# A decode attention kernel bound by its loads: paired transposes of K, other last parts of V, and the result on two partition quadrants

## The chip, the cores and the metric

The kernel runs on one core of one Trainium2 chip. The metric is the time on the device in microseconds (us); lower is better. All runs quoted here were timed beside runs of the kernel before on the same chip.

## The reference, cut to what matters

One decode step: attention of one new token over a long cache, plus a feed-forward block, for 4 batches and 32 heads.

```python
B, D, H, Sk, Dh, F = 4, 512, 32, 8192, 128, 1792        # all tensors bf16
xn = layernorm(x)                                       # x: [4, 1, 512]
q  = (xn @ wq) -> [B, H, 1, Dh]
p  = softmax(einsum("bhqd,bhkd->bhqk", q, k_cache) * Dh ** -0.5)
o  = einsum("bhqk,bhkd->bhqd", p, v_cache)              # k_cache, v_cache: [4, 32, 8192, 128]
return x + o @ wo + (silu(xn @ w_gate) * (xn @ w_up)) @ w_down
```

K and V are 268 MB each and every element is used once, so nearly all of the kernel is the reading of 551 MB.

## The kernel before: the parts concerned

There are 64 tiles of K and 64 of V, 4 MB each: one batch and two heads, with 128 rows of T = 128 keys. Five slots in SBUF, the on-chip memory, hold them. All loads go out on one queue. A round takes one K tile in eight pieces, and the V tile of two rounds earlier.

```python
def load_v(n, parts=(T,)):              # the last V tiles come in parts
    ...
    for w in parts:
        c1 = c0 + w * Dh
        nc.sync.dma_start(out=t_[:, c0:c1], in_=src[:, c0:c1])
        c0 = c1

def t_piece(n, g):                      # VectorE turns one eighth of a K tile
    w = TG * Dh
    kt = kt_pool.tile([P, w], dt.bfloat16, name="kt")
    src = k_tiles[n][:, g * w:(g + 1) * w].bitcast(dt.uint32)
    nc.vector.transpose(out=kt[:].bitcast(dt.uint32).rearrange(...), in_=src.rearrange(...))
    kts[n, g] = kt

def s_piece(n, g):                      # TensorE: scores, four matmuls per piece
    ...
    for jp in range(4):
        mm(s_ps[gr][:], zq[gr % 2][:, bb, jp, off:off + P], kt[:, jp // 2, :, jp % 2], ...)

def pv_last(xps, ts):                   # the last V tile: one small matmul per key column
    ...
def fin_2(j, xps, nb=B, start=True):    # adds the other three batches of the last head pair
    mm(xps[:, :, 0:nb], osb.pop(j)[:], rowy[:, :, 0:nb], start=start)

def wo_mm(i):                           # output projection of head i, halves in two PSUM banks
    for half in range(2):
        mm(yo_ps[half][0:B, :], otn[:, i, :], wo_t[0][:, i * D + half * DH:i * D + (half + 1) * DH], start=False)

# ... main loop over 66 rounds; cut: softmax, PV, feed-forward
load_v(nv, (32, 32, 32, 16, 16) if nv == NT - 1 else (32,) * 4 if nv == NT - 2 else (T,))
for g in range(NTG):
    t_piece(i, g)
    s_piece(i, g)
...
pv_last(xps, range(T // 2)); fin_2(...); pv_last(xps, range(T // 2, T)); fin_3(...)   # last round
...
nc.vector.tensor_copy(out=res[0][:], in_=yo_ps[0][0:B, :])
nc.sync.dma_start(out=out_flat[:, 0:DH], in_=res[0][:])
nc.scalar.copy(out=res[1][:], in_=yo_ps[1][0:B, :])
nc.scalar.dma_start(out=out_flat[:, DH:D], in_=res[1][:])
```

Of the kernel before, what the change touches and what calls it, by code (L numbers as in the profile page):

```python
# [8 lines left out]
dt = mybir.dt  # L9
# [6 lines left out]
def kernel(  # L16
# [13 lines left out]
    nc = tc.nc  # L30
    P = nc.NUM_PARTITIONS
# [10 lines left out]
    NT = M // HT  # L42
# [2 lines left out]
    NQ = P // QB  # L45
    TG = 16
    NTG = T // TG
    NV = 512 // Dh
    SLOT = T * Dh
    NSLOT = 5  # L50
# [11 lines left out]
    slots = ctx.enter_context(tc.tile_pool(name="slots", bufs=NSLOT))  # L62
    const = ctx.enter_context(tc.tile_pool(name="const", bufs=1))
    persist = ctx.enter_context(tc.tile_pool(name="persist", bufs=1))
    kt_pool = ctx.enter_context(tc.tile_pool(name="ktp", bufs=5))
    pp = ctx.enter_context(tc.tile_pool(name="pp", bufs=2))
    small = ctx.enter_context(tc.tile_pool(name="small", bufs=2))
    psS = ctx.enter_context(tc.tile_pool(name="psS", bufs=2, space=bass.MemoryType.PSUM))
    psO = ctx.enter_context(tc.tile_pool(name="psO", bufs=1, space=bass.MemoryType.PSUM))
    psM = ctx.enter_context(tc.tile_pool(name="psM", bufs=1, space=bass.MemoryType.PSUM))  # L70
    psX = ctx.enter_context(tc.tile_pool(name="psX", bufs=1, space=bass.MemoryType.PSUM))
    psY = ctx.enter_context(tc.tile_pool(name="psY", bufs=2, space=bass.MemoryType.PSUM))
    ctx.enter_context(tc.manual_schedule())

    def mm(out_ap, lhsT, rhs, start, **kw):
        nc.tensor.matmul(out_ap, lhsT=lhsT, rhs=rhs, start=start, stop=True,  # L76
                         skip_group_check=True, **kw)
# [125 lines left out]
    otn = persist.tile([P, H, B], dt.bfloat16, name="otn")  # L203

    DH = D // 2
    yo_ps = [psY.tile([B, DH], dt.float32, name="yo_ps") for _ in range(2)]
    ffn = {}

    def load_ffn():
# [9 lines left out]
    def do_ffn():  # L219
        wg, wu, wd = ffn["w"]  # L220

        gu_ps = psM.tile([P, 2, FC * B], dt.float32, name="mps")
        for i, w in enumerate((wg, wu)):
            for fc in range(FC):
                for c in range(EC):
                    mm(gu_ps[:, i, fc * B:(fc + 1) * B], w[:, c, fc:F:FC], xnt_w[:, c, 0:B],
                       start=(i == 0 and fc == 0 and c == 0))
        eg = persist.tile([P, FC * B], dt.float32, name="eg")
        nc.scalar.activation(out=eg[:], in_=gu_ps[:, 0, :], func=ACT.Exp, scale=-1.0)
        nc.vector.tensor_scalar(out=eg[:], in0=eg[:], scalar1=1.0, scalar2=None, op0=ALU.add)  # L230
        sig = persist.tile([P, FC * B], dt.float32, name="sig")
        nc.vector.reciprocal(out=sig[:], in_=eg[:])
        gs = persist.tile([P, FC * B], dt.float32, name="gs")
        nc.vector.tensor_tensor(out=gs[:], in0=gu_ps[:, 0, :], in1=sig[:], op=ALU.mult)
        ht = persist.tile([P, FC * B], dt.bfloat16, name="ht")
        nc.vector.tensor_tensor(out=ht[:], in0=gs[:], in1=gu_ps[:, 1, :], op=ALU.mult)
        yf_ps = psM.tile([B, D], dt.float32, name="mps")
        for fc in range(FC):
            mm(yf_ps[0:B, :], ht[:, fc * B:(fc + 1) * B], wd[:, fc, :], start=(fc == 0))
        nc.vector.tensor_tensor(out=yfx[:], in0=yf_ps[0:B, :], in1=xf[:], op=ALU.add)  # L240

        for j in range(2):
            mm(yo_ps[j][0:B, :], ident_f[0:B, 0:B], yfx[:, j * DH:(j + 1) * DH], start=True)



# [22 lines left out]
                out=zq[gr % 2][a * QB:(a + 1) * QB, :, :, XO + a * QB].rearrange("p b (j r) -> p r j b", r=2),  # L269
                in_=qt[a * QB:(a + 1) * QB, half, :, hh * 2:hh * 2 + 2, cg * B + bp * 2:cg * B + bp * 2 + 2])  # L270

    def t_piece(n, g):

        w = TG * Dh
        kt = kt_pool.tile([P, w], dt.bfloat16, name="kt")
        src = k_tiles[n][:, g * w:(g + 1) * w].bitcast(dt.uint32)
        nc.vector.transpose(out=kt[:].bitcast(dt.uint32).rearrange("p (j t r) -> p t j r", j=2, r=QB),  # L277
                            in_=src.rearrange("p (t j r) -> p t j r", j=2, r=QB))
        kts[n, g] = kt

    def s_piece(n, g):
        gr, bb = divmod(n, 2)
        if bb == 0 and g == 0:
            s_ps[gr] = psS.tile([P, 512], dt.float32, name="sps")
        kt = kts.pop((n, g))[:].rearrange("p (j n r) -> p j n r", j=2, r=2)
        off = XO - 2 * (bb * NTG + g)
        for jp in range(4):
            mm(s_ps[gr][:], zq[gr % 2][:, bb, jp, off:off + P], kt[:, jp // 2, :, jp % 2],
               start=(bb == 0 and g == 0 and jp == 0))
# [6 lines left out]
    def max_2(gr):  # L296

        mps = psM.tile([P, 512], dt.float32, name="mps")
        nc.tensor.matmul(mps[:, 0:P], lhsT=nmx.pop(gr)[:, 0:1].to_broadcast([P, P]), rhs=ident_f[:, :],  # L299
                         is_transpose=True, start=True, stop=True, skip_group_check=True)  # L300
        nm = small.tile([P, HT, 2], dt.float32, name="nm")
        nc.vector.tensor_reduce(out=nm[:], in_=by_row(mps[:, 0:P]), axis=AX.XY, op=ALU.max, negate=True)  # L302
        nc.vector.tensor_tensor(out=nm[:], in0=nm[:], in1=rowb_q[:], op=ALU.mult)
        nb = small.tile([P, 1], dt.float32, name="nb")
        nc.vector.reduce_sum(out=nb[:], in_=nm[:], axis=AX.XY)
        p_ = pp.tile([P, 512], dt.bfloat16, name="p_")
        rs = small.tile([P, 1], dt.float32, name="rs")
        nc.scalar.activation(out=p_[:], in_=s_ps.pop(gr)[:], func=ACT.Exp, bias=nb[:, 0:1], scale=qscale,
                             accum_out=rs[:])
        pt[gr] = p_  # L310
        rs_t[gr] = (rs, mps)
# [37 lines left out]
               start=(t == 0))  # L349

    def fin_1(j):
        o_sb = pp.tile([P, NV, Dh], dt.float32, name="o_sb")
        nc.scalar.copy(out=o_sb[:].rearrange("p u d -> p (u d)"), in_=o_acc[j % 2][:])  # L353
        nc.vector.tensor_tensor(out=o_sb[:], in0=o_sb[:], in1=rowu[:].unsqueeze(2).to_broadcast([P, NV, Dh]), op=ALU.mult)  # L354
        o1 = pp.tile([P, Dh], dt.float32, name="o1")
        nc.vector.reduce_sum(out=o1[:], in_=o_sb[:].rearrange("p u d -> p d u"), axis=AX.X)  # L356
        osb[j] = o1
# [20 lines left out]
                                    in1=r_[q0:q1, y, :].unsqueeze(1).to_broadcast([QB, 4, B]), op=ALU.mult)  # L378

    def wo_mm(i):  # L380
        for half in range(2):
            mm(yo_ps[half][0:B, :], otn[:, i, :], wo_t[0][:, i * D + half * DH:i * D + (half + 1) * DH], start=False)

    NK = T // NV
    JL = H // HT - 2
# [3 lines left out]
    for i in range(NT + LP):  # L389

        if i + 2 < NT:
            load_k(i + 2)
        nv = i + 2 - LP
        if 0 <= nv < NT:
            load_v(nv, (32, 32, 32, 16, 16) if nv == NT - 1 else (32,) * 4 if nv == NT - 2 else (T,))
        if i == R_FFN - 3:
            load_ffn()
        if i == R_FFN:
            do_ffn()
        if i == R_WO - 2:  # L400
            load_wo()
        gr, bb = divmod(i, 2)
        if i < NT:
            for g in range(NTG):
                t_piece(i, g)
                s_piece(i, g)
                if g == 0 and bb == 0 and gr > 0:
                    pt_turn(gr - 1)
            if bb == 1:
                if gr + 1 < NT // 2:  # L410
                    build_q(gr + 1)
                max_1(gr)
        elif i == NT:
            pt_turn(NT // 2 - 1)
        npv = i - LP
        if npv == NT - 1:
            xps = x_tile()
            pv_last(xps, range(T // 2))
            fin_2(H // HT - 1, xps, nb=B - 1, start=False)
            pv_last(xps, range(T // 2, T))  # L420
            fin_3(H // HT - 1, xps)
            wo_ready = H
        elif npv >= 0:
            for k in range(NK):
                pv_chunk(npv, k)
                if k == 4 and i < NT and bb == 1:
                    max_2(gr)
            jv, bv = divmod(npv, B)
            if bv % 2 == 0:
                row_sums(npv // 2)  # L430
            if bv == B - 1 or npv == NT - 2:
                fin_1(jv)
            if bv == B - 1:
                if jv < JL:
                    fin_q(jv)
                    if jv % 2 == 1:
                        wo_ready = (jv + 1) * HT
                else:
                    xps = x_tile()
                    fin_2(jv, xps)  # L440
                    fin_3(jv, xps)
                    wo_ready = (jv + 1) * HT
        elif i < NT and bb == 1:
            max_2(gr)
        if i >= R_WO:
            for _ in range(8):
                if wo_next < wo_ready:
                    wo_mm(wo_next)
                    wo_next += 1
# [2 lines left out]
        wo_next += 1  # L452
    assert wo_next == H

    res = [persist.tile([B, DH], dt.bfloat16, name=f"res{j}") for j in range(2)]
    nc.vector.tensor_copy(out=res[0][:], in_=yo_ps[0][0:B, :])
    nc.sync.dma_start(out=out_flat[:, 0:DH], in_=res[0][:])
    nc.scalar.copy(out=res[1][:], in_=yo_ps[1][0:B, :])
    nc.scalar.dma_start(out=out_flat[:, DH:D], in_=res[1][:])


# [1 line left out]
_INS = ['A_x', 'A_k_cache', 'A_v_cache', 'A_wq', 'A_wo', 'B_x', 'B_w_gate', 'B_w_up', 'B_w_down']  # L463
_OUTS = [((4, 1, 512), 'bfloat16')]
# [25 lines left out]
```

## Time and profile before

| quantity | before |
|---|---|
| time, median of 3 runs | 1288.93 us (1288.82 to 1289.4) |
| span of the profiled run, mean granted TensorE clock (1 is full speed) | 1287.1 us, 0.933 |
| TensorE busy, VectorE busy | 84%, 57% of the span |
| load queue | 99.4% of 16 DMA engines |
| transposes of K | 512, some 1.14 us apart |
| last piece of V lands | 1282.67 us |
| output issued, span ends | 1285.00, 1287.11 us |

Read it from the load queue. A queue that is full for 99.4% of the span leaves nothing to win in the middle.

### The profile page before, as it was taken

How to read it: one execution, taken by the hardware profiler on the slowest of the kernel's cores; microseconds unless marked ns; L12 is line 12 of the kernel's file. 1: busy time of each engine (PE TensorE's matmuls, PEld its weight loads, DVE VectorE, ACT ScalarE, POOL GpSimd, SP SyncE). 2: the span in 40 equal slices, each digit the busy share in tenths (PEclk: the TensorE clock that was granted, in tenths of full speed). 3: DMA queues.
4: the chain of work that ended last, by engine and by line, in shares of the span. 5: the costliest groups of instructions: out<-in, count | busy, mean ns of one | idle time of the engine just before them, and what ended most of it. 6: DMA issues, size and time to landing. Idle time of an engine off the chain costs nothing.

```text
span 1287.1 us, 11189 instructions
## 1 busy us (share of the span) xinstructions
PE 1083.1 (84%) x4778; PEld 430.3 (33%) x4778; DVE 738.1 (57%) x951; ACT 39.7 (3%) x87; POOL 5.3 (0%) x13
## 2 busy tenths in 40 slices
PE   4888888888888798897997888888887988978788
PEld 1334333333333333332333333333333333333334
DVE  6663556546556556466556566465465465573544
ACT  1000000000000000000000000000000000000000
POOL 1000000000000000000000000000000000000000
PEclk9898898998989999898998989989899898989899
DMA  9999999999999999999999999999999999999997
GB/s 407 427 430 435 437 425 437 429 436 431 432 435 428 436 432 433 431 432 435 431 435 428 434 432 431 436 431 433 430 434 431 437 430 432 433 431 427 433 434 304
DMA packets 21529, 551.49 MB, mean 428 GB/s; under 512 B 2268, under 2 KB 2792, under 8 KB 3944
## 3 DMA queue, kind: packets, MB, share of 16 engines
q1 hardware_dynamic: 21464, 550.78, 99.4%
q8 instruction: 37, 0.61, 0.2%
q14 instruction: 12, 0.10, 0.0%
q10 hardware_dynamic: 16, 0.01, 0.0%
HBM read 550.77 MB, written 0.00 MB: 428 GB/s over the span
## 4 chain that ended last, share of the span: by engine, by line
DMA 50%; PE 31%; DVE 14%; issue 5%; ACT 1%; SPq 0%; DVEq 0%
DMA slot<-in_A_k_cache_dram 44%; PE oacc L76 17%; PE sps L76 12%; DVE kt L277 11%; DMA slot<-in_A_v_cache_dram 6%; PE mps L76 1%; DVE ptz L318 1%; DVE o L356 1%; PE xps L76 1%; DVE o_sb L354 1%; ACT o_sb L353 0%; PE mps L299 0%; DVE otn L377 0%; PE yo_ps L76 0%; DVE rcp L328 0%
## 5 line engine op out<-in xcount | busy, mean ns | idle before, releaser
L76 PE MATMUL sps<-kt,zq 128*128 128x512 bf16 x2048 | 578.3, 421 | 145.2 <-DVE kt L277 128.7
L277 DVE STREAM_TRANSPOSE kt<-slot 128x1024 uint32<-128x1024 uint32 x512 | 587.6, 1210 | 90.4 <-DMA slot<-in_A_k_cache_dram 89.5
L76 PE MATMUL oacc<-slot,ptz 128*8 128x512 bf16 x2016 | 450.4, 379 | 0.4 <-DMA slot<-in_A_v_cache_dram 0.4
L76 PEld LDWEIGHTS <-zq 128*128 128x128 bf16 x2048 | 212.0, 104 | 496.1 <-issue 317.0
L76 PEld LDWEIGHTS <-ptz 128*8 128x8 bf16 x2016 | 177.5, 92 | 258.1 <-issue 27.8
L328 DVE RECIPROCAL rcp<-mps 128x4 f32<-128x4 f32 x32 | 5.9, 183 | 281.9 <-PE mps L76 281.9
L354 DVE TENSOR_TENSOR o_sb<-o_sb,rowu 128x512 f32<-128x512 f32 x16 | 11.1, 693 | 89.2 <-ACT o_sb L353 89.0
L76 PE MATMUL xps<-rowy,o 128*32 128x4 f32 (+1 forms) x228 | 13.5, 205 | 37.3 <-DVE o L356 37.3
L293 DVE TENSOR_REDUCE mx<-sps 128x1 f32<-128x512 f32 x32 | 22.1, 692 | 18.5 <-PE sps L76 18.5
L76 PEld LDWEIGHTS xps<-rowy,o 128*32 128x32 f32 (+1 forms) x228 | 12.1, 154 | 44.9 <-DVE o L356 44.9
L268 DVE COPY zq<-qt 32x8 bf16<-32x8 bf16 x128 | 21.3, 166 | 1.3
L302 DVE TENSOR_REDUCE nm<-mps 128x4 f32<-128x64 f32 x32 | 7.2, 225 | 24.0 <-PE mps L299 24.0
L356 DVE TENSOR_REDUCE o<-o_sb 128x128 f32<-128x512 f32 x16 | 16.3, 1020 | 0.5
L76 PEld LDWEIGHTS mps<-rowb,rs 128*128 128x128 f32 x64 | 9.5, 186 | 13.8 <-issue 13.8
L76 PEld LDWEIGHTS <-slot 128*128 128x128 bf16 x272 | 11.7, 126 | 3.5 <-DVE slot L188 2.6
L76 PE MATMUL mps<-rowb,rs 128*128 128x4 f32 x64 | 12.3, 263 | 0.0
L353 ACT COPY o_sb<-oacc 128x512 f32<-128x512 f32 x16 | 9.4, 586 | 76.8 <-PE oacc L76 76.8
L377 DVE TENSOR_TENSOR otn<-xps,rcp 32x16 bf16<-32x16 f32 x28 | 4.8, 170 | 11.7 <-PE xps L76 10.3
L299 PE MATMUL mps<-ident_f,mx 128*128 128x128 f32 x32 | 10.3, 323 | 0.8 <-DVE mx L293 0.8
L299 PEld LDWEIGHTS mps<-ident_f,mx 128*128 128x128 f32 x32 | 4.3, 133 | 14.7 <-DVE mx L293 14.2
L170 PE MATMUL xps<-ident,kt 4*128 4x4 bf16 x4 | 0.3, 173 | 10.1 <-DVE kt L165 10.1
L76 PE MATMUL yo_ps<-slot,otn 128*4 128x256 bf16 x64 | 8.2, 281 | 0.3 <-DVE otn L366 0.3
(150 smaller groups left out, 148.5 us busy)
## 6 DMA issues: line engine op xcount, KB each, us to landing
slot<-in_A_k_cache_dram SPq DMA_DIRECT2D x64, 4096.0 KB, 39.2
slot<-in_A_v_cache_dram SPq DMA_DIRECT2D x62, 4096.0 KB, 36.8
slot<-in_A_v_cache_dram SPq DMA_DIRECT2D x7, 1024.0 KB, 22.3
slot<-in_A_wq_dram SPq DMA_DIRECT2D x1, 4096.0 KB, 12.3
slot<-in_A_wo_dram SPq DMA_DIRECT2D x1, 3584.0 KB, 40.2
slot<-in_B_w_gate_dram SPq DMA_DIRECT2D x1, 1792.0 KB, 31.9
slot<-in_B_w_up_dram SPq DMA_DIRECT2D x1, 1792.0 KB, 35.8
slot<-in_B_w_down_dram SPq DMA_DIRECT2D x1, 1792.0 KB, 30.9
```

The lines of the kernel that those rows point to most:

```text
L76: nc.tensor.matmul(out_ap, lhsT=lhsT, rhs=rhs, start=start, stop=True, skip_group_check=True, **kw)
L268: nc.vector.tensor_copy(out=zq[gr % 2][a * QB:(a + 1) * QB, :, :, XO + a * QB].rearrange("p b (j r) -> p r j b", r=2), in_=qt[a * QB:(a + ...
L277: nc.vector.transpose(out=kt[:].bitcast(dt.uint32).rearrange("p (j t r) -> p t j r", j=2, r=QB), in_=src.rearrange("p (t j r) -> p t j r", ...
L293: nc.vector.reduce_max(out=mx[:], in_=s_ps[gr][:], axis=AX.X)
L299: nc.tensor.matmul(mps[:, 0:P], lhsT=nmx.pop(gr)[:, 0:1].to_broadcast([P, P]), rhs=ident_f[:, :], is_transpose=True, start=True, stop=True ...
L302: nc.vector.tensor_reduce(out=nm[:], in_=by_row(mps[:, 0:P]), axis=AX.XY, op=ALU.max, negate=True)
L318: nc.vector.transpose(out=t_[y * HP:(y + 1) * HP, :, y, :, :].rearrange("p s u x -> p s (u x)"), in_=p_[y * HP:(y + 1) * HP, :].rearrange( ...
L328: nc.vector.reciprocal(out=rcp[j][:, :, 2 * bp:2 * bp + 2], in_=mps[:, P:P + B].rearrange("p (y b) -> p y b", y=HT))
L353: nc.scalar.copy(out=o_sb[:].rearrange("p u d -> p (u d)"), in_=o_acc[j % 2][:])
L354: nc.vector.tensor_tensor(out=o_sb[:], in0=o_sb[:], in1=rowu[:].unsqueeze(2).to_broadcast([P, NV, Dh]), op=ALU.mult)
L356: nc.vector.reduce_sum(out=o1[:], in_=o_sb[:].rearrange("p u d -> p d u"), axis=AX.X)
L377: nc.vector.tensor_tensor(out=otn[q0:q1, blk * 4:blk * 4 + 4, :], in0=xps[q0:q1], in1=r_[q0:q1, y, :].unsqueeze(1).to_broadcast([QB, 4, B] ...
```

## The change

It does three things. VectorE transposes two pieces of K in one instruction (`ND = 2`; the last two tiles keep single pieces), with three K buffers of double size in place of five. The last-but-one V tile comes in two parts and the last one in parts that halve, so that the last part is small. The two halves of the result lie on two quadrants (of 32 partitions, `QB` in the code) of one bank of PSUM, the memory that matmuls write, so that their matmuls can overlap, and ScalarE and VectorE each copy half of the columns of both.

```diff
-    kt_pool = ctx.enter_context(tc.tile_pool(name="ktp", bufs=5))
+    kt_pool = ctx.enter_context(tc.tile_pool(name="ktp", bufs=3))
...
-    yo_ps = [psY.tile([B, DH], dt.float32, name="yo_ps") for _ in range(2)]
+    yo_ps = psY.tile([2 * QB, DH], dt.float32, name="yo_ps")
+    nc.vector.memset(yo_ps[:], 0.0)
+
+    def yo_mm(lhsT, rhs, start):
+        for a in range(2):
+            mm(yo_ps[a * QB:a * QB + B, :], lhsT, rhs[:, a * DH:(a + 1) * DH], start=start)
...
-    def t_piece(n, g):
+    def t_piece(n, g, nd):
         w = TG * Dh
-        kt = kt_pool.tile([P, w], dt.bfloat16, name="kt")
-        src = k_tiles[n][:, g * w:(g + 1) * w].bitcast(dt.uint32)
+        kt = kt_pool.tile([P, ND * w], dt.bfloat16, name="kt")
+        src = k_tiles[n][:, g * w:(g + nd) * w].bitcast(dt.uint32)
...                                  (one transpose of nd pieces; p_ and o_sb go to one buffer each)
-            load_v(nv, (32, 32, 32, 16, 16) if nv == NT - 1 else (32,) * 4 if nv == NT - 2 else (T,))
+            load_v(nv, (64, 32, 16, 8, 8) if nv == NT - 1 else (64, 64) if nv == NT - 2 else (T,))
...
-            for g in range(NTG):
-                t_piece(i, g)
-                s_piece(i, g)
+            nd = 1 if i >= NT - 2 else ND
+            for k in range(0, NTG, nd):
+                t_piece(i, k, nd)
+                for g in range(k, k + nd):
+                    s_piece(i, g)
...
-    nc.vector.tensor_copy(out=res[0][:], in_=yo_ps[0][0:B, :])
-    nc.scalar.copy(out=res[1][:], in_=yo_ps[1][0:B, :])
+    nc.scalar.copy(out=res[:, DH // 2:DH], in_=yo_ps[:, DH // 2:DH])
+    nc.vector.tensor_copy(out=res[:, 0:DH // 2], in_=yo_ps[:, 0:DH // 2])
```

More of the change, by code (lines that the diff above doesn't have):

```diff
@@ L47 @@
     NTG = T // TG
+    ND = 2
     NV = 512 // Dh
@@ L71 @@
     psX = ctx.enter_context(tc.tile_pool(name="psX", bufs=1, space=bass.MemoryType.PSUM))
-    psY = ctx.enter_context(tc.tile_pool(name="psY", bufs=2, space=bass.MemoryType.PSUM))
+    psY = ctx.enter_context(tc.tile_pool(name="psY", bufs=1, space=bass.MemoryType.PSUM))
     ctx.enter_context(tc.manual_schedule())
@@ L240, in do_ffn @@
         nc.vector.tensor_tensor(out=yfx[:], in0=yf_ps[0:B, :], in1=xf[:], op=ALU.add)
-        for j in range(2):
-            mm(yo_ps[j][0:B, :], ident_f[0:B, 0:B], yfx[:, j * DH:(j + 1) * DH], start=True)
+        yo_mm(ident_f[0:B, 0:B], yfx[:], True)
     NB4 = H // 4
@@ L270, in build_q @@
                 in_=qt[a * QB:(a + 1) * QB, half, :, hh * 2:hh * 2 + 2, cg * B + bp * 2:cg * B + bp * 2 + 2])
-    def t_piece(n, g):
+    def t_piece(n, g, nd):
         w = TG * Dh
-        kt = kt_pool.tile([P, w], dt.bfloat16, name="kt")
-        src = k_tiles[n][:, g * w:(g + 1) * w].bitcast(dt.uint32)
-        nc.vector.transpose(out=kt[:].bitcast(dt.uint32).rearrange("p (j t r) -> p t j r", j=2, r=QB),
+        kt = kt_pool.tile([P, ND * w], dt.bfloat16, name="kt")
+        src = k_tiles[n][:, g * w:(g + nd) * w].bitcast(dt.uint32)
+        nc.vector.transpose(out=kt[:, 0:nd * w].bitcast(dt.uint32).rearrange("p (j t r) -> p t j r", j=2, r=QB),
                             in_=src.rearrange("p (t j r) -> p t j r", j=2, r=QB))
-        kts[n, g] = kt
+        for i in range(nd):
+            kts[n, g + i] = kt[:, 0:nd * w].rearrange("p (j n r) -> p j n r", j=2, r=2)[:, :, i * 512:(i + 1) * 512, :]
     def s_piece(n, g):
@@ L284, in s_piece @@
             s_ps[gr] = psS.tile([P, 512], dt.float32, name="sps")
-        kt = kts.pop((n, g))[:].rearrange("p (j n r) -> p j n r", j=2, r=2)
+        kt = kts.pop((n, g))
         off = XO - 2 * (bb * NTG + g)
@@ L305, in max_2 @@
         nc.vector.reduce_sum(out=nb[:], in_=nm[:], axis=AX.XY)
-        p_ = pp.tile([P, 512], dt.bfloat16, name="p_")
+        p_ = pp.tile([P, 512], dt.bfloat16, name="p_", bufs=1)
         rs = small.tile([P, 1], dt.float32, name="rs")
@@ L351, in fin_1 @@
     def fin_1(j):
-        o_sb = pp.tile([P, NV, Dh], dt.float32, name="o_sb")
+        o_sb = pp.tile([P, NV, Dh], dt.float32, name="o_sb", bufs=1)
         nc.scalar.copy(out=o_sb[:].rearrange("p u d -> p (u d)"), in_=o_acc[j % 2][:])
@@ L380, in wo_mm @@
     def wo_mm(i):
-        for half in range(2):
-            mm(yo_ps[half][0:B, :], otn[:, i, :], wo_t[0][:, i * D + half * DH:i * D + (half + 1) * DH], start=False)
+        yo_mm(otn[:, i, :], wo_t[0][:, i * D:(i + 1) * D], False)
     NK = T // NV
@@ L403 @@
         if i < NT:
-            for g in range(NTG):
-                t_piece(i, g)
-                s_piece(i, g)
-                if g == 0 and bb == 0 and gr > 0:
+            nd = 1 if i >= NT - 2 else ND
[3 more added lines that the diff above has]
+                    s_piece(i, g)
+                if k == 0 and bb == 0 and gr > 0:
                     pt_turn(gr - 1)
@@ L453 @@
     assert wo_next == H
-    res = [persist.tile([B, DH], dt.bfloat16, name=f"res{j}") for j in range(2)]
-    nc.vector.tensor_copy(out=res[0][:], in_=yo_ps[0][0:B, :])
-    nc.sync.dma_start(out=out_flat[:, 0:DH], in_=res[0][:])
-    nc.scalar.copy(out=res[1][:], in_=yo_ps[1][0:B, :])
-    nc.scalar.dma_start(out=out_flat[:, DH:D], in_=res[1][:])
+    res = persist.tile([2 * QB, DH], dt.bfloat16, name="res")
+    nc.scalar.copy(out=res[:, DH // 2:DH], in_=yo_ps[:, DH // 2:DH])
+    nc.vector.tensor_copy(out=res[:, 0:DH // 2], in_=yo_ps[:, 0:DH // 2])
+    nc.sync.dma_start(out=out_flat[:, 0:DH], in_=res[0:B, :])
+    nc.scalar.dma_start(out=out_flat[:, DH:D], in_=res[QB:QB + B, :])
 _INS = ['A_x', 'A_k_cache', 'A_v_cache', 'A_wq', 'A_wo', 'B_x', 'B_w_gate', 'B_w_up', 'B_w_down']
```

## The prediction

> **What bounds the kernel now.** I read the page from its DMA part outwards, then the issues of loads, the groups, and last the end of the run, because a kernel that is bound by its loads can only be changed at its two ends.
>
> The DMA part of the page: packets and bytes, then each queue with packets, MB and share of 16 engines' span.
> ```profile
> DMA packets 21529, 551.49 MB, mean 428 GB/s; under 512 B 2268, under 2 KB 2792, under 8 KB 3944
> ...
> q1 hardware_dynamic: 21464, 550.78, 99.4%
> q8 instruction: 37, 0.61, 0.2%
> ...
> HBM read 550.77 MB, written 0.00 MB: 428 GB/s over the span
> ```
> The load queue alone fills 99.4% of the engines' span. A 32 KB packet takes 1.213 us in nearly every one of the 16,256 packet records, which is 432 GB/s for 16 engines; 550.8 MB at that rate is 1275 us of the 1287.1. There is no room in the middle. The issues (KB each, us from issue to landing) say whether the queue ever runs dry:
> ```profile
> slot<-in_A_k_cache_dram SPq DMA_DIRECT2D x64, 4096.0 KB, 39.2
> slot<-in_A_v_cache_dram SPq DMA_DIRECT2D x62, 4096.0 KB, 36.8
> ```
> One 4 MB load takes 4.19 MB / 432 GB/s = 9.7 us and lands 37 to 39 us after its issue, so about four loads are always queued: compute may be some us late without the DMA noticing.
>
> The groups (busy us, mean ns, then idle before and what ended it) show that compute is close behind, though:
> ```profile
> L76 PE MATMUL sps<-kt,zq 128*128 128x512 bf16 x2048 | 578.3, 421 | 145.2 <-DVE kt L277 128.7
> L277 DVE STREAM_TRANSPOSE kt<-slot 128x1024 uint32<-128x1024 uint32 x512 | 587.6, 1210 | 90.4 <-DMA slot<-in_A_k_cache_dram 89.5
> ```
> In a round (one K and one V tile, 19.4 us of DMA) eight transposes at 1.14 us set the pace of the K part, and VectorE waits for K only 89.5 us in 64 rounds, mostly some 5 us once in four rounds.
>
> The end, as stretches (busy us by engine, granted clock, DMA share, GB/s) and as the timeline (start, length, what):
> ```profile
> 1270.00:1275.00 5.00, 5.00 (x29) 2.17 (x28) 0.00 (x0) 0.00 (x0) 0.00 (x0) 1.00 1.00 418
> 1275.00:1280.00 5.00, 5.00 (x81) 3.06 (x79) 1.40 (x3) 0.59 (x1) 0.00 (x0) 1.00 0.56 236
> 1280.00:1288.00 8.00, 3.35 (x74) 2.42 (x70) 1.09 (x3) 0.36 (x1) 0.00 (x0) 0.58 0.10 38
> ```
> ```profile
> 1280.57 0.39 PE L76 MATMUL xps<-rowy,o 128*128 128x6 f32 x2 [0.49 <-DVE o L356]
> ...
> 1280.81 1.42 PE L76 MATMUL xps<-ptz,slot 128*128 128x2 bf16 x48
> ...
> 1282.71 0.59 PE L76 MATMUL xps<-ptz,slot 128*128 128x2 bf16 x16 [0.48 <-DMA slot<-in_A_v_cache_dram]
> 1283.34 0.17 DVE L366 TENSOR_TENSOR otn<-xps,rcp 128x8 bf16<-128x8 f32 x1 [2.83 <-PE xps L76]
> ...
> 1283.56 1.01 PE L76 MATMUL yo_ps<-slot,otn 128*4 128x256 bf16 x4 [0.26 <-DVE otn L366]
> 1284.40 0.41 DVE L456 CAST res<-yo_ps 4x256 bf16<-4x256 f32 x1 [0.89 <-PE yo_ps L76]
> 1284.61 0.36 ACT L458 CAST res<-yo_ps 4x256 bf16<-4x256 f32 x1 [5.89 <-PE yo_ps L76]
> ...
> 1285.00 0.28 ACTq L459 DMA_DIRECT2D out_dram<-res  x1
> ```
> From 1275 on only half of the DMA engines work. I linked the packets end to start into 16 engines: eight are done at 1274.5 to 1275.7, eight at 1280.4 to 1281.8. The 37 instruction fetches go round eight engines (their durations repeat with period 8), 37/8 = 4.6 each, and 7 us of lag / 5 fetches = 1.4 us each. So the last piece of V lands at 1282.67 because of instruction fetches, and what follows it is a serial tail of 4.4 us.
>
> **What the Trainium skill says.** "Runtime: NRT & Kernel Launch", Instruction fetch mechanics: instructions come in 16 KiB blocks of 256. The trace agrees: 0.61 MB / 37 = 16.4 KB, and TensorE's 2 x 4778 instructions / 256 = 37.3. The change leaves that count alone. "TensorEngine Tiling (Array Packing)", Key Properties: different column tiles can run at the same time. The trace agrees: the 32 projection matmuls of 512 columns onto four quadrants take 3.61 us (0.113 us each), while 32 PV matmuls of 512 columns onto one quadrant take 7.08 (0.22 each). "PSUM — Partial Sum Buffer", bank collisions: ScalarE and VectorE must not read one bank and quadrant at once, and software has to keep them apart; before, the two result halves sat in two banks, so no run shows it yet. "DMA: Bandwidth & Descriptors", Where 436 GB/s comes from: a ceiling of 435 GB/s at the ports; the trace shows 432.
>
> **The change, part by part.**
> Two pieces in one transpose: 512 transposes become 62 x 4 + 2 x 8 = 264. I estimate one of 128x2048 at 2.25 us (twice the pitch of 1.144, from 8.01 us for seven, less some 0.04 of start). VectorE's busy time so falls by roughly 10 to 20 us of 738, none of it on the path of the loads. The cost is granularity: TensorE gets its first K piece 1.1 us later, and behind the last transpose it has 8 matmuls left instead of 4, 4 x 0.213 = 0.85 us more, less about 0.1 for the earlier end of the transposes: PV starts about 0.75 us later in a round. Four rounds add some 3 us where 5 are free, and four loads are queued, so the middle stays as it is. It matters once: the last four rounds run on without a long wait. Tile 60 starts when its K lands (1195.28), and its matmuls run at half clock, so the larger pieces hide there (0.1). Tile 61 passes on +0.75; tiles 62 and 63 are single pieces again and pass it on. So fin_2, at 1280.57 now, comes near 1281.4.
>
> Other last V parts: tile 62 is 16 packets of 16 KB on each DMA engine instead of 32 of 8 KB. At 309 ns for 8 KB and 159 for 4 KB, 9 ns are fixed; 32 x 309 = 9.89 us becomes 16 x 609 = 9.74, so -0.15. Tile 63: 3 x 8 x 309 + 2 x 8 x 159 = 9.96 becomes 8 x (609 + 309 + 159 + 84 + 84) = 9.96. The last part lands near 1282.5. Behind it are 8 matmuls instead of 16: 8 x 0.0265 = 0.21 us less, if TensorE is not late. But with fin_2 0.8 later it has all of the second half (64 matmuls, 64 x 0.0265 + 0.17 = 1.87 us) still to do from about 1281.6: it ends at 1283.5, not at 1283.30: +0.2. The arrival of V is then no longer the last wait.
>
> Result on two quadrants: the four last matmuls start 0.17 to 0.21 us apart (half clock). As two overlapping pairs they end two steps earlier: -0.4. The other 60 are hidden.
>
> Copies: each engine does 128 columns on 64 partitions rather than 256 on 4. ScalarE: 0.586 us for 512 columns and 0.362 for 256 give 0.25 for 128; VectorE 0.27 in the same way. But both read one bank, so I expect ScalarE first and VectorE after it: 0.04 + 0.25 + 0.03 + 0.27 + 0.03 = 0.62 us from the last matmul to the output's issue, where 0.43 is now: +0.2. If they overlap it is -0.1.
>
> Sum: +0.2 - 0.4 + 0.2 = 0.0. A clear gain in the last matmuls pays for a later TensorE and a serial copy. Smaller DMA packets count and a possible overlap pull a little below: I take -0.1, so 1288.8.
>
> **The rivals.** First: TensorE is not late at the end (VectorE's doubled instruction is as fast as 2.15, or it gains elsewhere). Then the landing of V sets the end: 1282.5 + 0.05 + 0.38 = 1282.95, -0.35, and with -0.4 and +0.2 the sum is -0.55, or -0.85 with overlapping copies: 1288.1 to 1288.4. For it: 0.48 us of idle before the last 16 matmuls. Against: TensorE is 97% busy from 1240 to 1270. Second: the pieces of 2.25 us make TensorE's gaps longer and its clock drops to half in more stretches (mean granted clock is 0.933 now, 0.50 in 1282 to 1288). Half clock over one stretch of 3.4 us of the last rounds costs 1.7 us: 1290.5. For it: it drops today after gaps of 1.4 to 2.5 us, and TensorE's gap before tile 61 grows to 1.6 us. Third: the middle becomes bound by compute, were a round to grow by over 1.3 us; then loads are issued late, and up to 5 us may be lost. Against it: four loads in the queue. Fourth: VectorE's instruction fetches fall from about 9 to 7, and a DMA engine that ends last is relieved; against: their 8 KB packets take 0.309 us and the engines that end last agree within 0.15 us, so I give it nothing.
>
> **Range and chances.** Runs of before spread over 0.6 us, and my terms are each uncertain by 0.2 to 0.4; the first rival gives the low side, half of the second the high one: 1287.8 to 1290.0. 2% is 26 us, and no rival reaches that: same 0.98.
>
> **What would show it.** Right: load queue still above 99%, 37 fetches, V landing within 0.3 us of 1282.5, about 264 transposes of 2.2 to 2.3 us, TensorE's idle time on them no smaller, last four matmuls near 0.6 us, VectorE's cast starting after ScalarE's. Wrong: the last piece of V landing elsewhere by over 1 us (then fetches moved), a clock well under 0.93, a K wait near zero, or time to landing well below 37 us (compute bound).

## The result, and the profile after

| | before | after |
|---|---|---|
| median of 6 runs | 1288.91 us (1288.78 to 1289.4) | 1289.12 us (1288.67 to 1289.89) |
| ratio | | 1.0002, 95% interval 0.9989 to 1.0014: same |
| span of the profiled run, clock | 1287.1 us, 0.933 | 1286.9 us, 0.925 |

A ratio here is the mean time of one kernel's fast runs over that of the other's of the same rounds, so it is not quite the ratio of the medians. The interval is 0.13% wide on either side, 1.6 us; what follows on tenths of a microsecond is read from single traces and not from the times.

The DMA part of the page after (queue, packets, MB, share of 16 engines' span):
```profile
q1 hardware_dynamic: 21176, 550.78, 99.4%
q8 instruction: 37, 0.61, 0.2%
q14 instruction: 9, 0.07, 0.0%
```
and of the page before, the one line that the prediction left out:
```profile
q14 instruction: 12, 0.10, 0.0%
```
The load queue is as full as before, with 288 packets fewer from the larger V parts. TensorE's 37 instruction fetches (q8) are the same. The fetches on q14 fell from 12 to 9 as VectorE's instructions fell from 951 to 704; they turn out to matter below.

The groups after (busy us, mean ns, idle before and what ended it), and the issues of the large loads (KB each, us from issue to landing):
```profile
L77 PE MATMUL sps<-kt,zq 128*128 128x512 bf16 x2048 | 553.5, 421 | 174.2 <-DVE kt L283 172.0
L283 DVE STREAM_TRANSPOSE kt<-slot 128x2048 uint32<-128x2048 uint32 (+1 forms) x264 | 572.5, 2217 | 56.8 <-DMA slot<-in_A_k_cache_dram 55.9
```
```profile
slot<-in_A_k_cache_dram SPq DMA_DIRECT2D x64, 4096.0 KB, 38.7
slot<-in_A_v_cache_dram SPq DMA_DIRECT2D x62, 4096.0 KB, 37.1
```
There are 264 transposes; the mean of 2217 ns mixes in the 16 small ones, and the mean record of a pair is 2.28 us; in a row one starts every 2.22 us (8.87 / 4, below). VectorE's wait for K fell from 89.5 to 55.9 us and TensorE's wait for the transposes rose from 128.7 to 172.0: compute has lost part of its slack, and the loads did not notice, since they are issued as early as before.

Tile 61, one of the last paired ones, on the timeline of before (start us, length us, what):
```profile
1214.75 9.11 DVE L277 STREAM_TRANSPOSE kt<-slot 128x1024 uint32<-128x1024 uint32 x8
...
1224.91 1.25 PE L76 MATMUL oacc<-slot,ptz 128*8 128x512 bf16 x5
```
and of after:
```profile
1214.41 8.87 DVE L283 STREAM_TRANSPOSE kt<-slot 128x2048 uint32<-128x2048 uint32 x4
...
1225.23 1.25 PE L77 MATMUL oacc<-slot,ptz 128*8 128x512 bf16 x5
```
Four paired transposes take 8.87 us where eight took 9.11. From the first transpose to the first PV matmul it is 1224.91 - 1214.75 = 10.16 us before and 1225.23 - 1214.41 = 10.82 after, 0.66 more: the matmuls of a whole pair are left behind the last transpose.

The end of the run after, on the timeline (in brackets: idle time before it, and what ended that):
```profile
1280.94 0.39 PE L77 MATMUL xps<-rowy,o 128*128 128x6 f32 x2 [0.54 <-DVE o L363]
...
1281.18 1.83 PE L77 MATMUL xps<-ptz,slot 128*128 128x2 bf16 x64
1283.05 0.17 DVE L373 TENSOR_TENSOR otn<-xps,rcp 128x8 bf16<-128x8 f32 x1 [2.16 <-PE xps L77]
...
1283.27 0.59 PE L77 MATMUL yo_ps<-slot,otn 128*4 128x256 bf16 x4 [0.26 <-DVE otn L373]
1283.90 0.26 ACT L465 CAST res<-yo_ps 64x128 bf16<-64x128 f32 x1 [4.81 <-PE yo_ps L77]
1284.19 0.28 DVE L466 CAST res<-yo_ps 64x128 bf16<-64x128 f32 x1 [0.98 <-ACT res L465]
1284.51 0.35 SPq L467 DMA_DIRECT2D out_dram<-res  x1
```
The 64 matmuls of the second half of V run in one go, with no wait for V among them; before, 48 ran and the last 16 waited. The four output matmuls take 0.59 us, where they took 1.01. VectorE's copy waits for ScalarE's. Step by step, from the two traces:

| step, us | before | after | difference |
|---|---|---|---|
| last piece of V lands | 1282.67 | 1282.25 | -0.42 |
| fin_2 starts | 1280.57 | 1280.94 | +0.37 |
| last matmul of the second half ends | 1283.30 | 1283.01 | -0.29 |
| last four matmuls, length | 1.01 | 0.59 | -0.42 |
| from their end to the last issue of the output | 0.43 | 0.65 | +0.22 |
| last issue of the output | 1285.00 | 1284.51 | -0.49 |
| from there to the end of the span | 2.11 | 2.39 | +0.28 |
| end of the span | 1287.11 | 1286.90 | -0.21 |

So the last microseconds gain half a microsecond, and more than half of that is given back behind the output's issue. Two questions were left. Why did V land 0.42 earlier and not 0.15? And is the tail the only place where this kernel can be moved?

### The profile page after: what moved, and what is told of

It reads as the page before. It is cut to its first block, busy times and chain, and to the rows that moved or that the text cites. A ratio compares the mean times of both kernels' runs of the same rounds, so it can differ in the third digit from the quotient of the medians.

```text
span 1286.9 us, 10820 instructions
## 1 busy us (share of the span) xinstructions
PE 1053.8 (82%) x4778; PEld 427.0 (33%) x4778; DVE 722.2 (56%) x704; ACT 39.6 (3%) x87; POOL 5.3 (0%) x13
## 2 busy tenths in 40 slices
DMA packets 21238, 551.46 MB, mean 429 GB/s; under 512 B 2236, under 2 KB 2760, under 8 KB 4040
## 3 DMA queue, kind: packets, MB, share of 16 engines
q1 hardware_dynamic: 21176, 550.78, 99.4%
## 4 chain that ended last, share of the span: by engine, by line
DMA 48%; PE 31%; DVE 18%; issue 3%; ACT 0%; SPq 0%; DVEq 0%; ACTq 0%
DMA slot<-in_A_k_cache_dram 48%; PE oacc L77 18%; DVE kt L283 16%; PE sps L77 11%; PE mps L77 1%; DVE ptz L325 1%; PE xps L77 0%; DVE o L363 0%; PE mps L306 0%; DVE o_sb L361 0%; ACT o_sb L360 0%; DVE rcp L335 0%; DVE yfx L247 0%; PE yo_ps L77 0%; DVE sig L239 0%
## 5 line engine op out<-in xcount | busy, mean ns | idle before, releaser
L77 PE MATMUL sps<-kt,zq 128*128 128x512 bf16 x2048 | 553.5, 421 | 174.2 <-DVE kt L283 172.0
L283 DVE STREAM_TRANSPOSE kt<-slot 128x2048 uint32<-128x2048 uint32 (+1 forms) x264 | 572.5, 2217 | 56.8 <-DMA slot<-in_A_k_cache_dram 55.9
L77 PE MATMUL mps<-xnt_w,slot 128*128 128x4 bf16 x112 | 6.8, 199 | 0.3 <-DVE rcp L335 0.3
```

Of the source, the lines that this page charges most:

```text
L77: nc.tensor.matmul(out_ap, lhsT=lhsT, rhs=rhs, start=start, stop=True, skip_group_check=True, **kw)
L283: nc.vector.transpose(out=kt[:, 0:nd * w].bitcast(dt.uint32).rearrange("p (j t r) -> p t j r", j=2, r=QB), in_=src.rearrange("p (t j r) -> ...
```

## The experiments

**Theory A** was the prediction's: the eight DMA engines that serve TensorE's instruction fetches end up to 7 us late and set the end of the loads. **Theory B** was its fourth rival, there given nothing: the fetches on q14 count too. **Theory C** was a plain one: more work or other timing on TensorE moves the end, whatever the fetches. Ten kernels ran. For "linked packets" below, each load packet was joined to the one that starts where it ends on the same engine, which gives 16 chains; where two engines are in step a link can go to the wrong one, so only the ends of chains and clean ones are used.

### One part at a time: the result on two quadrants (quad_only)

```diff
 before.py
-    yo_ps = [psY.tile([B, DH], dt.float32, name="yo_ps") for _ in range(2)]
+    yo_ps = psY.tile([2 * QB, DH], dt.float32, name="yo_ps")
...            (yo_mm, the memset and the copies as in the change; nothing else)
```

> The kernel before with only the result on two quadrants (and its two copies). My theory, that the parts of the change cancel at the end: the four last matmuls take 0.6 us instead of 1.0, the two copies one after the other take 0.2 us longer, V lands as before, so the output is issued about 2.1 us after the last piece of V instead of 2.33, and the time is 0.2 us lower, 1288.7. Rival, that nothing behind the landing of V counts because other things move more: no difference in the time, but also none in the tail.

Measured: 1289.05 us median (1288.59 to 1289.55, 5 runs) beside 1288.75 (9 runs), ratio 1.0, interval 0.9988 to 1.0013. On its timeline the four matmuls took 0.59 us, as in the change, and the copies were serial again:
```profile
1283.82 0.59 PE L76 MATMUL yo_ps<-slot,otn 128*4 128x256 bf16 x4 [0.26 <-DVE otn L371]
```
But they began 0.26 us later than before. The clock records show why: TensorE ran at half clock until 1204.48 and again from 1235.2 to 1242.03, where before it was at full clock from 1202.74 to 1281.25. fin_2 came at 1281.49, 0.92 late, and V's arrival no longer mattered. The half-clock stretches are multiples of 3.41 us (here 6.83), which agrees with the two clock states and the window of 3.4 us in the Trainium skill, "TensorE: Matmul & The Clock Gate", What's actually happening; they differ from run to run of like kernels, which by itself makes some tenths of difference between single runs. The gain of 0.42 us exists, and one such stretch covers it.

### One part at a time: the paired transposes (pair_only)

```diff
 before.py
+    ND = 2
...            (t_piece, s_piece, the loop and the buffers as in the change; nothing else)
```

> The kernel before with only the doubled transposes (and the buffers that they need). My theory: VectorE's waits for K fall from 89 to about 56 us, since each round of compute is longer, and the loads do not notice; from the first transpose of tile 61 to its first PV matmul it takes 10.8 us instead of 10.16, fin_2 comes some 0.4 to 0.8 us later, and the time grows by 0.0 to 0.4 us. Rival, that larger instructions free VectorE and so help: the time falls.

Measured: 1288.85 us (1288.33 to 1288.88, 5 runs), ratio 0.9998, interval 0.9986 to 1.0011. The parts of V are as before here, and yet V landed at 1282.25, as in the whole change:
```profile
1280.97 0.59 PE L77 MATMUL xps<-rowy,o 128*128 128x6 f32 x2 [0.54 <-DVE o L358]
1281.41 1.85 PE L77 MATMUL xps<-ptz,slot 128*128 128x2 bf16 x64
```
So the earlier landing comes from the transposes, which move not one byte of V. What they share with it is the instruction fetches: q14 shows 9 in this page, as in the change. fin_2 was at 1280.97, within 0.03 of the change.

### One part at a time: the parts of V (vparts_only)

```diff
 before.py
-            load_v(nv, (32, 32, 32, 16, 16) if nv == NT - 1 else (32,) * 4 if nv == NT - 2 else (T,))
+            load_v(nv, (64, 32, 16, 8, 8) if nv == NT - 1 else (64, 64) if nv == NT - 2 else (T,))
```

> The kernel before with only the other last parts of V. My theory: 8 matmuls behind the last piece instead of 16, and the piece lands 0.15 us earlier: 0.3 us less in the tail, the output is issued about 2.1 us after the landing. Rival, that smaller pieces cost more on the DMA engines: the last piece lands later than 1282.7.

Measured: 1288.9 us (1288.62 to 1289.18, 5 runs), ratio 0.9999, interval 0.9987 to 1.0012. V landed at 1282.72, no earlier than before (1282.67), with 12 fetches on q14. The 0.15 us that fewer and larger packets were to bring is not seen. A small last part does help behind the landing, though:
```profile
1281.01 2.13 PE L76 MATMUL xps<-ptz,slot 128*128 128x2 bf16 x64
1283.18 0.17 DVE L366 TENSOR_TENSOR otn<-xps,rcp 128x8 bf16<-128x8 f32 x1 [2.58 <-PE xps L76]
```
The matmuls end 0.42 us after the landing (1283.14), where before they ended 0.63 after it (1283.30 - 1282.67). That is the eight matmuls that the prediction counted as 0.21.

### Fewer instructions on TensorE (few_instr)

This kernel computes a wrong sum on purpose: one of four score matmuls and one of four PV chunks. Its loads are those of before. The comparison with the reference passed it all the same, so that is no evidence that its numbers are right.

```diff
 before.py
-        for jp in range(4):
+        for jp in range(1):
...
-            for k in range(NK):
+            for k in range(0, NK, 4):
```

> Wrong result on purpose: a quarter of the matmuls with K and a quarter of those with V (but for the last tile), all loads as before. TensorE's instructions fall from 9556 to about 3460, its fetches from 37 to 13 or 14. My theory, that the fetches on eight DMA engines set when the last piece of V lands: the most that one engine has falls from 5 to 2, the two groups of DMA engines end 2.8 us apart instead of 7, and the time falls by 4 us, to about 1285. Rival, that the engines differ for another reason, and the fetches only ride on those: the last piece lands near 1282.7 as before, and the time falls by under 0.7 us, which is what a faster TensorE can save behind it.

Measured: 1287.86 us (1287.61 to 1288.11, 4 runs), ratio 0.9992, interval 0.9976 to 1.0007. That is a miss: 0.9 us came where theory A expected almost four. The page and the stretches of the end (busy us by engine, clock, DMA share, GB/s) say where theory A was incomplete:
```profile
q8 instruction: 13, 0.21, 0.1%
q14 instruction: 11, 0.09, 0.0%
```
```profile
1270.00:1275.00 5.00, 2.37 (x35) 1.43 (x35) 1.65 (x3) 0.58 (x1) 0.00 (x0) 0.67 0.97 407
1275.00:1280.00 5.00, 2.53 (x73) 2.35 (x70) 0.27 (x1) 0.00 (x0) 0.00 (x0) 0.50 0.27 110
```
From 1275 to 1280 the DMA share is 0.27, where it was 0.56 before: most of the late engines are now done early, as theory A said. But in the linked packets one engine ends alone, at 1281.21; the next is done at 1277.64. In the trace of before the engine that ends last (1282.37) has nine gaps of some 0.30 us in its load packets, each with a load packet beside it that takes 0.53 us longer, and at each stands an 8 KB packet of q14. Nine times 0.84 us is 7.6 us. (The other three of the 12 packets on q14 stand beside load packets that are only 0.24 to 0.28 us longer.) TensorE's fetches look different: 1.42 us each, four or five on each of eight engines, ending at 1280.4 to 1282.10. So two things are late by nearly the same amount and hide each other: eight engines by 37 fetches of TensorE, and one by nine fetches of another engine, which the counts tie to VectorE (951 instructions and nine such packets before, 704 and six in the change). In few_instr eight of the nine are left, so that most of its small gain is this one fetch: 0.84 of the 1.16 us by which the last engine ended earlier. Why it is one fewer, with as many VectorE instructions on the page, was not found.

The prediction argued against this from the 8 KB packets' own duration of 0.309 us. That was the wrong number: the engine loses the gap, in which that packet stands, and the 0.53 us of the longer packet after it.

### Fewer instructions on both (few_both)

If that is right, taking VectorE's fetches away as well must give what few_instr failed to give. Again a wrong sum on purpose: few_instr, and only the first of the eight transposes of each K tile.

```diff
 few_instr
-                t_piece(i, g)
+                if g == 0:
+                    t_piece(i, g)
...            (and all matmuls of the tile read that one piece)
```

> Wrong result on purpose: few_instr, and besides only one transpose of eight in each K tile (all matmuls of the tile read that piece). VectorE's instructions fall from some 1190 to 361, its fetches from 9 to 3; TensorE's are 13 or 14 as in few_instr. My theory: the engine that takes VectorE's fetches no longer ends last (3 x 0.84 = 2.5 us), nor do those of TensorE's (2 x 1.42 = 2.8 us): the last piece of V lands near 1278, 4.5 us earlier than before and 3.3 earlier than in few_instr, and the time is near 1284.3. Rival, that the engine which ended alone at 1281.2 in few_instr is slow for another reason: as few_instr, 1287.9.

Measured: 1284.58 us (1284.3 to 1284.68, 4 runs) beside 1288.88 (9 runs), ratio 0.9967, interval 0.9951 to 0.9982. Expected was about 1284.3, and 4.3 us is eleven times the spread of its own runs. q14 shows 8 packets, and the last wait for V ends 4.4 us earlier than before:
```profile
q14 instruction: 8, 0.06, 0.0%
```
```profile
1278.33 0.59 PE L76 MATMUL xps<-ptz,slot 128*128 128x2 bf16 x16 [0.65 <-DMA slot<-in_A_v_cache_dram]
```
All 16 engines are done by 1277.97. Of the 8 packets seven are of 8 KB: the three of the cheaper kind, and four of VectorE's, where few_instr has eight and the expectation said three. Four fewer at 0.84 us are 3.4 us, and the step from few_instr to few_both is 3.3 us for the transposes alone, although the loads are the same and neither kernel waits for VectorE at the end.

### More instructions on TensorE (more_instr), with a control (same_time)

Both are quad_only with matmuls into a spare PSUM bank in each of the first 61 rounds. more_instr adds 34 tiny ones (2 columns), same_time adds 4 large ones (512 columns): similar time on TensorE with few instructions.

```diff
 quad_only
+        if i < NT - 3:
+            for _ in range(34):                                            # same_time: range(4)
+                mm(idle_ps[:, 0:2], ident[:], idle_in[:, 0:2], start=True)  # same_time: 512 columns
...            (the tiles idle_ps and idle_in; the comments are not in the kernels)
```

> The result on two quadrants as in quad_only, with 34 tiny matmuls (2 columns, into a PSUM bank that nobody reads) added in each of the first 61 rounds: 2074 matmuls, 4148 more TensorE instructions, so 53 or 54 fetches instead of 37. What few_instr left: eight DMA engines take TensorE's fetches in turn at 1.42 us each, and a ninth takes all of VectorE's at 0.84 us each. My theory: the most that one engine has rises from 5 to 7, the last piece of V lands 2.5 us later, the time is 1291.4 to 1291.9. Rival, that fetches do not delay the loads: no change over 0.5 us, as TensorE is given 0.9 us more per round and has more than 1.2 to spare.

> The control of more_instr: the same 0.9 us of TensorE per round in 4 matmuls of 512 columns, 488 more instructions, 39 fetches, so that no DMA engine has more than 5. My theory: within 0.4 us of quad_only, 1288.6 to 1289.4. Rival, that TensorE's time and not its instructions is what more_instr shows: as much slower as more_instr.

Measured: more_instr 1291.28 us (1291.13 to 1293.16, 4 runs), ratio 1.0022, interval 1.0009 to 1.0036; same_time 1289.58 (1288.88 to 1291.03, 4 runs), ratio 1.0009, interval 0.9993 to 1.0024; beside 1288.77 (9 runs). The pages, more_instr first:
```profile
q8 instruction: 53, 0.87, 0.2%
```
```profile
q8 instruction: 39, 0.64, 0.2%
```
With 16 more fetches, four engines end at 1284.53 to 1284.71 and four at 1283.06 to 1283.35, which fits seven and six fetches each: the means are 1.4 us apart for one more. The last piece of V lands at 1284.98, 2.5 us later than in quad_only (1282.47), as expected. With two more fetches the late engines end at 1280.43 to 1282.35, as before, and V lands at 1282.65. more_instr was a little below the expected 1291.4 to 1291.9; same_time was half a microsecond above quad_only, with a wide spread, and 0.2 above its expected range. Theory C would have had both alike; theory A and the fetches stand. The times of the two nearly touch (1291.13 at least, 1291.03 at most), so this rests on the landings. same_time is too loose to exclude that TensorE's time costs a microsecond of its own.

### Loads cut unevenly (uneven)

If the engines are uneven because of fetches, the bytes might be shared to match: 40 of the 128 columns of the last-but-one V tile were loaded as 119 partitions and 9, so that the engines that end early get more. By the rule of the Trainium skill, "DMA: Bandwidth & Descriptors", Why a DMA increments its semaphore by 16 and not by 1, on how many engines a transfer uses (the largest divisor up to 16), 119 partitions go to seven. The trace agrees: a full load has 16 packets of 4 bytes, one for each engine, and two partial loads and a full one in place of four full ones leave 32 fewer small packets (2236 under 512 B, 2268 before), so the two partial loads have 16 between them, 7 and 9.

```diff
 before.py
-            load_v(nv, (32, 32, 32, 16, 16) if nv == NT - 1 else (32,) * 4 if nv == NT - 2 else (T,))
+            load_v(nv, (32, 32, 32, 16, 16) if nv == NT - 1 else (-40, 88) if nv == NT - 2 else (T,))
...            (a negative width: partitions 0 to 118 and 119 to 127 in two loads)
```

> The kernel before, but 40 of the 128 columns of the last but one V tile are loaded as 119 and 9 partitions. If a load of 119 partitions is cut into 7 equal parts, seven DMA engines take 17 rows each of 10 KB and most of the others none. If those seven are among the engines without fetches, the engines with fetches are relieved by 8 rows, 3 us, and the time falls by 2.5 to 3 us; if they are among the engines with fetches, the time grows by 3 to 4 us. Rival theory, that the end does not hang on the last DMA engine: no change.

Measured: 1305.94 us (1305.11 to 1306.21, 4 runs), ratio 1.0132, interval 1.0118 to 1.0146: 17 us slower, and no theory had expected that. The stretches of the end, with the same columns as above:
```profile
1270.00:1275.00 5.00, 5.00 (x16) 1.59 (x15) 1.88 (x5) 0.78 (x2) 0.00 (x0) 0.66 0.99 231
1275.00:1280.00 5.00, 3.69 (x18) 1.38 (x15) 0.08 (x1) 0.00 (x0) 0.00 (x0) 1.00 0.98 209
```
The DMA engines are 98 to 99% busy and move half of what they should. While the packets of the partial loads move, from 1254.8 to 1281.8, every other packet is slow too: 8 KB took 571 ns (median) in place of 309, and 32 KB 2.30 us in place of 1.21. From 1282.2 on, 8 KB packets are back at 309. The last V landed at 1298.80. Why a partial load slows the packets beside it was not found; it stays open. The idea is not usable in this form.

### The halves in two banks (two_banks)

Is the serial copy at the end due to the shared bank? This is the changed kernel with each half in its own bank, still on two quadrants, each copied by one engine.

```diff
 after.py
-    yo_ps = psY.tile([2 * QB, DH], dt.float32, name="yo_ps")
+    yo_ps = [psY.tile([2 * QB, DH], dt.float32, name="yo_ps") for _ in range(2)]
...
-    nc.scalar.copy(out=res[:, DH // 2:DH], in_=yo_ps[:, DH // 2:DH])
-    nc.vector.tensor_copy(out=res[:, 0:DH // 2], in_=yo_ps[:, 0:DH // 2])
+    nc.vector.tensor_copy(out=res[0:B, :], in_=yo_ps[0][0:B, :])
+    nc.scalar.copy(out=res[QB:QB + B, :], in_=yo_ps[1][QB:QB + B, :])
```

> The kernel after, but the two halves of the result lie in two PSUM banks (still on two quadrants), each copied by one engine, 256 columns of 4 partitions, as before. My theory: the copies of 0.41 and 0.36 us run side by side, the output is issued some 0.45 us after the last matmul instead of 0.65, and the time is 0.1 to 0.2 us under the kernel after, too little for the rounds to show; the trace shows it. Rival, that the two copies in the kernel after do not wait for each other because of the bank: then they run one after the other here too.

Measured: 1288.56 us (1288.49 to 1288.89, 5 runs) beside 1288.77, ratio 0.9998, interval 0.9986 to 1.0011. Its timeline:
```profile
1284.00 0.41 DVE L464 CAST res<-yo_ps 4x256 bf16<-4x256 f32 x1 [0.68 <-PE yo_ps L77]
1284.03 0.36 ACT L465 CAST res<-yo_ps 4x256 bf16<-4x256 f32 x1 [4.83 <-PE yo_ps L77]
```
Both copies now wait for TensorE alone and run side by side. From the last matmul to the last issue it is 0.48 us and no longer 0.65, although each copy is longer. The overlap of the matmuls is kept (1283.37 to 1283.96). So two quadrants in two banks do better than two quadrants in one. This agrees with the Trainium skill, "PSUM — Partial Sum Buffer", PSUM bank collisions, by which software keeps ScalarE and VectorE from one bank and quadrant: with one bank the copies ran one after the other (0.26 and 0.28 us), with two side by side (0.41 and 0.36 us, 0.03 apart). But each engine now also reads a quadrant of its own and writes other partitions of `res`; one bank with a quadrant for each engine was not run, so the bank alone is not isolated.

### A shorter end (shorter_tail)

In the changed kernel TensorE is late and V's arrival is not. two_banks, with single transposes for the last four tiles and not two, and with three quarters of the last V tile's matmuls before fin_2 and not half:

```diff
 two_banks
-            nd = 1 if i >= NT - 2 else ND
+            nd = 1 if i >= NT - 4 else ND
...
-            pv_last(xps, range(T // 2))
+            pv_last(xps, range(3 * T // 4))
...
-            pv_last(xps, range(T // 2, T))
+            pv_last(xps, range(3 * T // 4, T))
```

> The kernel after with the two halves of the result in two banks, single transposes in the last four rounds instead of two, and the earlier batches' part of the last tile (fin_2) put behind three quarters of the last V tile's matmuls instead of one half. My theory: V lands near 1282.3 as in the kernel after; then 8 matmuls remain, not a queue of 64 that begins at 1281.2, so the last of them ends near 1282.7 instead of 1283.0, the output is issued near 1284.1 instead of 1284.5 (before: 1285.0), and the time is 0.4 to 0.9 us under both kernels. Rival, that a half clock in the last rounds, which comes and goes, decides: within 0.3 us of the others.

Measured: 1287.99 us (1287.87 to 1288.15, 5 runs) beside 1288.88 (1288.65 to 1289.63, 9 runs), ratio 0.9993, interval 0.9981 to 1.0006. By the 2% measure it is the same, and the interval includes 1; but each of its five runs lies below each run of before in its own rounds, and below each run of the change (lowest 1288.67, other rounds). The timeline shows what changed:
```profile
1281.01 0.98 PE L77 MATMUL xps<-ptz,slot 128*128 128x2 bf16 x24
1282.27 0.38 PE L77 MATMUL xps<-ptz,slot 128*128 128x2 bf16 x8 [0.28 <-DMA slot<-in_A_v_cache_dram]
```
Eight matmuls are left after the landing at 1282.22, and V's arrival is the last wait again. The output is issued at 1283.97, 0.54 us earlier than in the change.

## Why the prediction was right or wrong

The prediction of "same" held: no term is larger than half a microsecond out of 1289. 1289.12 lies inside 1287.8 to 1290.0, 0.3 above 1288.8; the profiled runs differ by -0.2. Neither difference can be told from zero by the times.

**Loads bound all, and the middle stays.** Right. The load queue is at 99.4%, TensorE has 37 fetches, and the loads land 37 to 39 us after issue, all as the prediction had asked. VectorE's busy time fell by 15.9 us, inside the 10 to 20 expected, and none of it is in the time. The gap before each fourth K tile shrank from some 5.3 to 2.9 us, so 2.4 of it was spent where 3 was expected. Rival 3 did not come.

**What sets the landing of V.** Incomplete. TensorE's fetches make eight engines late, at 1.4 us each; more_instr shows that. But the engine that ended last before was another one, with nine fetches of 0.84 us, and few_instr missed for that reason. The prediction named this as its fourth rival (9 fetches to 7; it was 9 to 6) and gave it nothing, because it misread the ends of the engines in the trace of before: it saw eight late ones whose last agree within 0.15 us, but nine are late, and the last three end at 1281.76, 1282.10 and 1282.37. Its own line hints at it: a DMA share of 0.56 from 1275 to 1280 is nine engines of 16. The change took three of those nine fetches away. In after, pair_only, two_banks and shorter_tail one of the nine late engines then ends at 1279.53 to 1279.71, which fits 3 x 0.84 = 2.5 us less, and TensorE's late engines, up to 1281.90 in the change, became the last. The term of the sum was -0.15, from fewer packets. It measured -0.42, and for another cause: pair_only has it, vparts_only has not.

**Later TensorE.** The mechanism was right and the size was off. Tile 61 passed on 0.66 us, expected 0.75. Tile 60 cost 0.34 where 0.1 was expected (from its first transpose to that of tile 61, 19.47 us before and 19.81 after). TensorE ran its 64 matmuls in one go, with V no longer the last wait; that was the step's claim. But fin_2 came at 1280.94 and not near 1281.4, so the term measured -0.29 at the last matmul where +0.2 was expected. This is the largest error in the sum. The reason is in the start of tile 60, before and after:
```profile
1195.28 1.25 DVE L277 STREAM_TRANSPOSE kt<-slot 128x1024 uint32<-128x1024 uint32 x1 [15.94 <-DMA slot<-in_A_k_cache_dram]
```
```profile
1194.60 2.31 DVE L283 STREAM_TRANSPOSE kt<-slot 128x2048 uint32<-128x2048 uint32 x1 [13.42 <-DMA slot<-in_A_k_cache_dram]
```
Its K landed 0.68 us earlier, where the prediction had held that time fixed. It is early in every kernel with paired transposes (1194.46 to 1194.80 in pair_only, two_banks, after and shorter_tail) and late in those without pairs that keep all fetches (1195.08 to 1195.39 in quad_only, vparts_only and before). That it is again the relieved DMA engine fits two other pairs of runs: the same wait ends at 1190.88 in few_both and at 1193.28 in few_instr, with fewer fetches for VectorE, and at 1197.49 in more_instr and 1195.25 in same_time, with more for TensorE.

**Last four matmuls.** Right: -0.42, expected -0.4, and the same 0.59 us in quad_only, two_banks and shorter_tail.

**Serial copies.** Right: +0.22, expected +0.2, VectorE after ScalarE. In two_banks, with a bank and a quadrant for each engine, the wait is gone.

**What was not in the sum.** The output is issued 0.49 us earlier and the span ends only 0.21 earlier. The traces split the 0.28 us. From the last landing to the end it is 0.06 more (0.96, before 0.89): fewer V loads moved the outputs to earlier semaphores of SyncE's list of final checks, and one more check follows. From the last issue to the last landing it is 0.22 more (1.43, before 1.22). That goes with the result on two quadrants: in the six kernels that have it the two outputs are issued within 0.012 us and the last lands 1.35 to 1.43 us later; in the six others they are 0.16 us apart and it is 1.20 to 1.22. Whether the common issue or the layout costs it, no run separates.

**The sum.** -0.29 - 0.42 + 0.22 + 0.28 = -0.21, where 0.0 had been the sum and -0.1 was taken. The error of 0.5 in one term and the unseen 0.28 partly cancel. That the total was closer than its parts is luck.

**The other rivals.** The first, TensorE not late, did not come in the change, and shorter_tail, which makes it so, comes to about the time that it named (1287.99, named 1288.1 to 1288.4), with the copies side by side and fewer matmuls left after fin_2. The second, half clock, came in small form: stretches of 3.41 or 6.83 us near 1235 appear in pair_only, vparts_only, two_banks and quad_only, none between 1202.8 and 1281.2 in the profiled runs of before and after.

## What to carry to other kernels

When loads fill the queue for 99% of the span, look at each DMA engine's own end and not at their mean: instruction fetches land on some of them, and what seems a change of compute can move the loads through the number of instructions. Where two causes end within a few tenths of a microsecond of each other, removing one shows almost nothing, so remove both before you say that a theory has failed. And when two engines are to read a result at the end, put their halves in different PSUM banks (0.17 us here, seen in the trace and too little for the times).

## What the Trainium skill lacked or had wrong

- "Runtime: NRT & Kernel Launch", Instruction fetch mechanics, calls the cost of crossing a block "mostly hidden". It is not hidden from a full load queue: a fetch of TensorE delays a DMA engine by 1.42 us, 16 more of them end the loads 2.3 us later than before (the last engine at 1284.71 and not 1282.37), and with fewer on TensorE and VectorE the kernel is 4.3 us faster. The page does not say that they are spread unevenly: TensorE's go round eight engines, and those tied to VectorE fall on one, by the ends of the engines.
- The same section gives 16 KiB for the blocks of every engine. TensorE's agree (0.61 MB / 37 = 16.5 KB). The nine on q14 that the counts tie to VectorE are of 8 KB and cost 0.84 us each.
- "DMA: Bandwidth & Descriptors", on how many engines a transfer uses, does not say that a load on fewer engines can slow the others: while one load of 119 partitions and one of 9 moved, packets of 8 KB took 571 ns (309 otherwise), and the time was 1305.94 us. The cause was not found.
